# Rearranging the warm-up, the first output tile and the weight loads of a fused attention and feed-forward kernel

## The chip, the cores and the metric

The kernel runs on one core of a Trainium2 chip. The metric is the device time of one execution in microseconds; four runs of the kernel before gave a median of 228.43 us (228.22 to 228.93). The profiled execution is one of these runs.

## The reference

A linear attention with decay (batch 4, 8 heads, 768 positions, head size 64) is followed by a gated feed-forward network (FFN). All inputs and the output are float32.

```python
for b in range(nb):                                  # blocks of 64 positions
    intra = einsum('bhic,bhjc->bhij', qb, kb) * Dmask    # lam ** (i - j), i >= j
    intra = einsum('bhij,bhjd->bhid', intra, vb)
    inter = einsum('bhid,bhde->bhie', qb * lam_pow, kv_state)
    out[:, :, sl] = intra + inter
    kv_state = lam_block * kv_state + einsum('bhsd,bhse->bhde', kb * rev_pow, vb)
x = out.transpose(0, 2, 1, 3).reshape(3072, 512)
g = x @ w_gate                                       # 512 x 1536
return (silu(g) * (x @ w_val)) @ w_out               # 1536 x 512
```

## The kernel before, in words

The 3072 rows of x are worked in six tiles of 512 rows. A tile is two *groups*; a group is 256 positions of one batch element with all heads, so there are twelve groups, 0 to 11. The attention of a group runs ahead of the tile that uses it, in between the FFN's matmuls.

**A group's attention.** `load_group` issues the transfers of k, q and v on SP's queue (`load_fp32`, L93; groups 6 and later in 64-element rows). `cast_scaled` (L255) casts k on ScalarE and scales q on VectorE (in group 3 on GpSimd, called POOL in the profile), and then issues a transposing DMA on SP (`dma_transpose`, L251), which makes the tile qkt. Groups 0 to 2 are transposed on TensorE instead (`pe_transpose`). `v_scale` (L238) makes v_s on GpSimd. On TensorE, `upd_mm` (L382) multiplies k with v_s for the state, `scores` (L326, or L352 from group 6 on) multiplies k with q, `inter` in `core_a` (L461) multiplies q with the state, and `intra` in `core_b` (L474) multiplies the masked scores with v_s. ScalarE copies the update out (`upd_copy`, L404), GpSimd adds it to the state (`state`, L421 to L432), VectorE masks the scores (L333, L357). The masks wait in a list, `later`, and are issued one or two at a time by `run_later` after an FFN step. `guard` (L445) is a tiny ScalarE copy between `inter` and `intra`; `evac` (L486) casts the result into xt, the FFN's input, by default both halves on ScalarE. `ahead(g)` is update and scores of a group; `attend(g)` is `core_a(g)`, then update and scores of the next group, then `core_b(g)`.

**The FFN.** One *step* handles 128 of the 1536 columns: four matmuls for the gate (L514), Silu on ScalarE into a tile sil (L518, three buffers), four matmuls for val (L528) and the product on VectorE into h (L531). Steps of tile 0 and tile 1 are partly halved: 256 rows (`b0` to `b1`) at a time, since the second group comes later. `ffn_out(t, b)` is the last product for 128 rows: twelve matmuls (L547), a copy on ScalarE into osb and a transfer on ScalarE's queue (L549, L550). For the very last one the 512 columns are cut in two: the first half goes over ScalarE, the second over VectorE and SP's queue.

**Weights.** `w_piece` loads pieces of w_gate and w_val, `wo_piece` two row blocks of w_out (512 KB), all on SP's queue and in float32 buffers that they share with k and q (tag raw, ten buffers). `w_cast` and `wo_cast` cast them to bfloat16.

**What sets the order.** Each engine runs its instructions in the order in which they were issued. The order is written out by hand: `step` appends an FFN step to a list, `at(n, fn, ...)` adds a call behind step n, and a loop (L766) issues the steps with their calls. In it, s0 are the steps of tile 0 (from the third on), s1a and s1b those of the two halves of tile 1, sn those of a later tile. PSUM has eight banks that `bank()` hands out in turn, so a bank comes round at every eighth request, and TensorE must wait if the bank's last reader hasn't finished. At the start TensorE is given matmuls on constants (`warm_up`, L130, and `warm_into`, L167), around the product that spreads lam over the partitions (L163), from which ScalarE makes all decay tables by Ln and Exp.

In the kernel before, all of w_out's six pieces are requested behind `s1a[3]`; group 5 is cast behind `s1b[3]`; the outputs of tile 0 stand behind `s1b[11]`, with the attention of group 5 between them, ahead of tile 2:

```python
    at(s1b[11], ffn_out, 0, 0)
    at(s1b[11], ahead, 5)
    at(s1b[11], run_later, 3)
    at(s1b[11], ffn_out, 0, 1)
    at(s1b[11], core_a, 5)
    at(s1b[11], ffn_out, 0, 2)
    at(s1b[11], core_b, 5)
```

Tile 2 then holds the outputs of tile 1, and each later tile those of the one before it.

Of the kernel before, what the change touches and what calls it, by code (L numbers as in the profile page):

```python
# [9 lines left out]
BF16 = mybir.dt.bfloat16  # L10
# [27 lines left out]
def _body(ctx, tc, nc, q, k, v, lam, moe_w_gate, moe_w_val, moe_w_out, out):  # L38
    B, H, S, D = q.shape
    HP = H // 2  # L40
    BLK = 128
    NBLK = S // BLK
    DM = H * D
    DFF = moe_w_gate.shape[1]
    MC = DM // 128
    FC = DFF // 128
    NG = NBLK * B // 2
    M = BLK // 2

# [20 lines left out]
    h_pool = ctx.enter_context(tc.tile_pool(name="h", bufs=2))  # L70
# [8 lines left out]
    def bank():  # L79
        b = banks[ring[0] % 8]  # L80
        ring[0] += 1
        return b
# [8 lines left out]
    st = {}  # L91
# [54 lines left out]
    for b2 in range(2):  # L146
        ps = slice(b2 * M, b2 * M + M)
# [4 lines left out]
    for b2 in range(2):  # L152
        ps = slice(b2 * M, b2 * M + M)
# [5 lines left out]
           for b in range(B)]  # L159

    lam_ps = bank()
    warm_up(4)
    nc.tensor.matmul(lam_ps[:, 0:H], ones[:, 0:128], lam_row, start=True, stop=True)  # L163
    warm_up(3)
    def warm_into(b, n, cols=256):
        for _ in range(n):
            nc.tensor.matmul(b[:, 0:cols], warm[:, 0:128], warm[:, 0:cols], start=True, stop=True)  # L167
# [32 lines left out]
    wv_sb = wpool.tile([128, MC, DFF], BF16, name="wv_sb")  # L200
    wo_sb = wpool.tile([128, FC, DM], BF16, name="wo_sb")
    wg_d = moe_w_gate.rearrange("(c p) f -> p c f", p=128)
# [315 lines left out]
        nc.scalar.activation(sil[:, 0:N], gp[:, 0:N], AF.Silu)  # L518

    def ffn_val(t, fc, b0=0, b1=B):  # L520
        if ("h", t) not in st:
            st[("h", t)] = h_pool.tile([128, FC, B, BLK], BF16, name="h", tag="h")
        h_sb, xt, sil = st[("h", t)], st[("xt", t)], st[("sil", t, fc, b0)]
# [7 lines left out]
        nc.vector.tensor_tensor(out=h_sb[:, fc, b0:b1].rearrange("p b n -> p (b n)"),  # L531
                                in0=sil[:, 0:N], in1=vp[:, 0:N], op=ALU.mult)

    def ffn_fc(t, fc, b0=0, b1=B):
# [1 line left out]
        ffn_val(t, fc, b0, b1)  # L536

    def ffn_out(t, b, last=False):
        h_sb = st[("h", t)]
        osb = osb_pool.tile([128, DM], FP32, name="osb", tag="osb")  # L540
        row = groups[2 * t + b // 2][0] * S + (groups[2 * t + b // 2][1] * 2 + b % 2) * BLK
        halves = ((0, DM // 2, nc.scalar.copy, nc.scalar), (DM // 2, DM, nc.vector.tensor_copy, nc.sync)) \
            if last else ((0, DM, nc.scalar.copy, nc.scalar),)
        for c0, c1, fn, eng in halves:
            ps = bank()[:, 0:c1 - c0]
            for fc in range(FC):
                nc.tensor.matmul(ps, h_sb[:, fc, b], wo_sb[:, fc, c0:c1],  # L547
                                 start=(fc == 0), stop=(fc == FC - 1))
            fn(out=osb[:, c0:c1], in_=ps)  # L549
            eng.dma_start(out=bass.AP(tensor=out.tensor, offset=out.offset + row * DM + c0,  # L550
                                      ap=[[DM, 128], [1, c1 - c0]]),
                          in_=osb[:, c0:c1])
# [3 lines left out]
        upd(g)  # L556
        scores(g)

    def attend(g):
        run_later(len(later))  # L560
        core_a(g)
        if g + 1 < NG:
            upd_mm(g + 1)
            upd_copy(g + 1)
            scores(g + 1)
            late, later[:] = later[:], []
        core_b(g)
# [160 lines left out]
    at(s1b[6], run_later, 2)  # L728
    at(s1b[6], wo_cast)
    at(s1b[6], wo_cast)  # L730
    at(s1b[6], v_scale, 5, nc.gpsimd)
    at(s1b[8], wo_cast)
    at(s1b[9], core_a, 4)
    at(s1b[10], core_b, 4)
    at(s1b[10], wo_cast, ACTC)
    at(s1b[11], ffn_out, 0, 0)
    at(s1b[11], ahead, 5)
    at(s1b[11], run_later, 3)
    at(s1b[11], ffn_out, 0, 1)
    at(s1b[11], core_a, 5)  # L740
    at(s1b[11], ffn_out, 0, 2)
    at(s1b[11], core_b, 5)
    at(s1b[11], cast_scaled, 6)
    at(s1b[11], load_group, 7)
    at(s1b[11], v_scale, 6, nc.gpsimd)
    at(s1b[11], ffn_out, 0, 3)

    outs = [(1, b) for b in range(4)]
    for t in range(2, NG // 2):
        sn = [step(t, fc) for fc in range(FC)]  # L750
        if t == 2:
            at(sn[2], ahead, 6)
        for j, g in ((3 if t == 2 else 0, 2 * t + 3), (7 if t == 2 else 6, 2 * t + 4)):
# [10 lines left out]
        outs = [(t, b) for b in range(4)]  # L764

    for n, (t, fc, b0, b1) in enumerate(steps):  # L766
        if t >= 1 and t + 1 < NG // 2 and ("xt", t + 1) not in st:
# [5 lines left out]
            if fn in (attend, ahead):  # L773
                run_later(1)
    run_later(len(later))
    for t, b in outs:
        ffn_out(t, b, last=(b == 3))
# [1 line left out]
_INS = ['q', 'k', 'v', 'lam', 'moe_w_gate', 'moe_w_val', 'moe_w_out']  # L779
_OUTS = [((3072, 512), 'float32')]  # L780
# [25 lines left out]
```

## Time and profile before

| | |
|---|---|
| median of 4 runs | 228.43 us |
| the profiled execution | 228.93 us |
| its span, first to last instruction | 227.2 us |
| mean granted clock of TensorE | 0.999 |
| TensorE matmuls busy | 218.1 us, 96% of the span |
| ScalarE, GpSimd, VectorE busy | 107.0, 90.0, 89.3 us |
| moved by DMA | 39.70 MB, mean 175 GB/s |

In the profile PE is TensorE, PEld its weight loads, ACT ScalarE, DVE VectorE, POOL GpSimd, SP SyncE, which issues most transfers. L12 is line 12 of the kernel. A busy row gives the busy time of each engine and its instructions; the row of digits cuts the span in 40 slices of 5.68 us, 9 being 90% busy or more. A line of waits gives who waited for whom, and then the total in us, the number of waits and the longest. A line of the chain or of the timeline begins with the start and the duration in us; in the timeline, brackets give the engine's idle time ahead of the instruction and what ended it.

### The profile page before, as it was taken

Reading aid. Unit: us, or ns where it says so; the run is one execution under the profiler, and the core shown is the slowest. Engines: PE = TensorE matmul, PEld = TensorE weight load, DVE = VectorE, ACT = ScalarE, POOL = GpSimd, SP = SyncE. Lnnn points to the kernel's source line nnn. Section 1 sums busy time; section 2 is a strip of 40 time slices with the busy share of each in tenths; the row PEclk is TensorE's granted clock in tenths of the full one; section 3 lists DMA queues with packets and bytes.
Section 4 is the critical chain, followed back from the end, with each engine's and each line's share of the span. In section 5 each row is a group of like instructions: output and inputs, shape, how many; then the busy total and the mean of one; then the engine's idle time right before and its main releaser. Section 6 shows DMA issues by size and latency. Waiting matters only on the chain.

```text
span 227.2 us, 5890 instructions
## 1 busy us (share of the span) xinstructions
PE 218.1 (96%) x2431; PEld 118.2 (52%) x2443; DVE 89.3 (39%) x151; ACT 107.0 (47%) x209; POOL 90.0 (40%) x131
## 2 busy tenths in 40 slices
PE   8789998999998999999999999999999999999994
PEld 3556455878864444454544544544544444444443
DVE  2664357585835214545353362253242123222200
ACT  5878584754662446363354463453433423322221
POOL 6675737732595132978292092092150000000000
PEclk9999999999999999999999999999999999999999
DMA  6999999999997778799977748815101101101122
GB/s 196 345 358 372 367 324 306 229 220 328 349 263 183 203 166 214 185 204 198 225 162 185 189 95 208 218 39 138 49 3 48 46 3 46 46 0 46 49 92 92
DMA packets 88012, 39.70 MB, mean 175 GB/s; under 512 B 57650, under 2 KB 83506, under 8 KB 87986
## 3 DMA queue, kind: packets, MB, share of 16 engines
q1 hardware_dynamic: 83474, 32.64, 54.6%
q10 hardware_dynamic: 4512, 6.69, 8.3%
q8 instruction: 19, 0.31, 0.6%
q14 instruction: 7, 0.06, 0.1%
HBM read 28.31 MB, written 6.29 MB: 152 GB/s over the span
## 4 chain that ended last, share of the span: by engine, by line
PE 73%; DMA 11%; POOL 7%; SPq 5%; issue 1%; ACT 0%; DVE 0%; DVEq 0%; POOLq 0%
PE bank L547 27%; PE bank L514 21%; PE bank L528 20%; DMA v<-in_v_dram 5%; SPq L99 4%; DMA wraw<-in_moe_w_val_dram 4%; DMA woraw<-in_moe_w_out_dram 3%; POOL v_s L238 3%; POOL wo_sb L232 2%; PE bank L474 2%; PE bank L461 2%; PE bank L382 1%; POOL kvf L421 1%; PE bank L352 1%; SPq L227 1%
## 5 line engine op out<-in xcount | busy, mean ns | idle before, releaser
L531 DVE TENSOR_TENSOR h<-sil,bank 128x512 bf16<-128x512 bf16 (+1 forms) x87 | 51.4, 595 | 109.5 <-PE bank L528 93.8
L514 PE MATMUL bank<-xt,wg_sb 128*128 128x512 bf16 (+1 forms) x348 | 76.6, 343 | 0.0
L528 PE MATMUL bank<-xt,wv_sb 128*128 128x512 bf16 (+1 forms) x348 | 76.4, 342 | 0.0
L518 ACT ACTIVATE sil<-bank 128x512 bf16<-128x512 f32 (+1 forms) x87 | 45.9, 527 | 44.2 <-PE bank L514 41.3
L547 PE MATMUL bank<-wo_sb,h 128*128 128x512 bf16 (+1 forms) x288 | 64.3, 370 | 1.5 <-POOL wo_sb L232 0.8
L528 PEld LDWEIGHTS <-wv_sb 128*128 128x128 bf16 x348 | 33.9, 98 | 28.4 <-POOL wv_sb L221 0.3
L514 PEld LDWEIGHTS <-wg_sb 128*128 128x128 bf16 x348 | 32.4, 98 | 27.2 <-DVE xt L486 0.3
L547 PEld LDWEIGHTS <-h 128*128 128x128 bf16 x300 | 29.1, 98 | 33.3 <-issue 1.1
L549 ACT COPY osb<-bank 128x512 f32<-128x512 f32 (+1 forms) x24 | 13.9, 577 | 54.8 <-PE bank L547 52.8
L238 POOL TENSOR_TENSOR v_s<-v,dec 128x1024 bf16<-128x1024 f32 (+1 forms) x14 | 23.3, 1667 | 13.0 <-DMA v<-in_v_dram 9.9
L421 POOL TENSOR_TENSOR kvf<-kvs,ups 128x256 f32<-128x256 f32 x8 | 5.8, 726 | 44.0 <-ACT ups L404 44.0
L333 DVE TENSOR_TENSOR ssb<-bank,causal 128x512 bf16<-128x512 f32 x24 | 15.3, 682 | 3.7 <-PE bank L326 3.6
L486 ACT CAST xt<-bank 128x512 bf16<-128x512 f32 x21 | 12.8, 665 | 2.9 <-PE bank L474 2.4
L430 POOL CAST kvn<-kvf 64x256 bf16<-64x256 f32 x24 | 13.5, 563 | 1.5
L421 POOL TENSOR_TENSOR kvf<-kvf,ups 128x256 f32<-128x256 f32 x16 | 12.6, 787 | 0.6
L404 ACT COPY ups<-bank 128x256 f32<-128x256 f32 (+1 forms) x24 | 9.5, 449 | 2.4 <-PE bank L382 1.5
L258 ACT CAST qk<-kraw 128x1024 bf16<-128x1024 f32 x9 | 9.4, 1043 | 0.0
L260 DVE TENSOR_TENSOR qk<-qraw,qdn 128x1024 bf16<-128x1024 f32 x6 | 7.5, 1255 | 4.1 <-DMA qraw<-in_q_dram 4.1
L357 DVE TENSOR_TENSOR ssb<-bank,causaln 128x512 bf16<-128x512 f32 x12 | 8.2, 687 | 1.2 <-PE bank L352 1.0
L221 POOL CAST wv_sb<-wraw 128x1024 bf16<-128x1024 f32 (+1 forms) x6 | 5.8, 970 | 5.6 <-DMA wraw<-in_moe_w_val_dram 5.4
L232 POOL CAST wo_sb<-woraw 128x1024 bf16<-128x1024 f32 x5 | 5.2, 1043 | 6.3 <-DMA woraw<-in_moe_w_out_dram 6.3
L474 PE MATMUL bank<-ssb,v_s 64*64 64x128 bf16 (+1 forms) x384 | 6.8, 208 | 0.5 <-ACT guard L445 0.5
(63 smaller groups left out, 117.0 us busy)
## 6 DMA issues: line engine op xcount, KB each, us to landing
out_dram<-osb ACTq DMA_DIRECT2D x23, 256.0 KB, 2.1
v<-in_v_dram SPq DMA_DIRECT2D x16, 256.0 KB, 4.5
woraw<-in_moe_w_out_dram SPq DMA_DIRECT2D x6, 512.0 KB, 7.0
kraw<-in_k_dram SPq DMA_DIRECT2D x24, 128.0 KB, 3.3
qraw<-in_q_dram SPq DMA_DIRECT2D x24, 128.0 KB, 3.4
wraw<-in_moe_w_gate_dram SPq DMA_DIRECT2D x5, 512.0 KB, 6.8
wraw<-in_moe_w_val_dram SPq DMA_DIRECT2D x5, 512.0 KB, 7.0
kraw<-in_k_dram SPq DMA_DIRECT2D x4, 512.0 KB, 7.6
```

The costliest lines, as they stand in the source:

```text
L238: eng.tensor_tensor(out=st[("vs", g)][:, h0:h1], in0=st[("v", g)][:, h0:h1].rearrange("p h (s d) -> p h s d", s=2), in1=vfac(g, h0, h1), o ...
L333: nc.vector.tensor_tensor(out=ssb[:, h2, 2 * c:2 * c + 2].rearrange("p a s n -> p a (s n)"), in0=sp[(c, h2)].rearrange("p (a x) -> p a x", ...
L421: nc.gpsimd.tensor_tensor(out=o, in0=f, in1=u, op=ALU.add)
L430: nc.gpsimd.tensor_copy(out=o[64 - h2 * 64:128 - h2 * 64], in_=f[h2 * 64:h2 * 64 + 64])
L474: nc.tensor.matmul(op[r][h2 * 64:h2 * 64 + 64, cols(g, hp, s)], v_s[ps, 2 * hp + h2, s], ssb[ps, h2, hp * 2 + s] if g >= NAT0 else ssb[ps, ...
L486: fns[r](out=xt[:, g % 2, :, r].rearrange("p h (m s) -> p h s m", s=2) if g < NAT0 else xt[:, g % 2, :, :, r * M:r * M + M], in_=op[r].rea ...
L514: nc.tensor.matmul(gp[:, 0:N], wg_sb[:, mc, fs], xt[:, b0 // 2:b1 // 2, mc].rearrange("p g b n -> p g (b n)"), start=(mc == 0), stop=(mc = ...
L518: nc.scalar.activation(sil[:, 0:N], gp[:, 0:N], AF.Silu)
L528: nc.tensor.matmul(vp[:, 0:N], wv_sb[:, mc, fs], xt[:, b0 // 2:b1 // 2, mc].rearrange("p g b n -> p g (b n)"), start=(mc == 0), stop=(mc = ...
L531: nc.vector.tensor_tensor(out=h_sb[:, fc, b0:b1].rearrange("p b n -> p (b n)"), in0=sil[:, 0:N], in1=vp[:, 0:N], op=ALU.mult)
L547: nc.tensor.matmul(ps, h_sb[:, fc, b], wo_sb[:, fc, c0:c1], start=(fc == 0), stop=(fc == FC - 1))
L549: fn(out=osb[:, c0:c1], in_=ps)
```

## The change

Seven edits are made together.

1. The four 512-column matmuls ahead of lam's product become 78 matmuls of 64x64 weights and 8 columns, alternating between the upper and the lower half of the array. Five instead of three wide ones follow.
2. v of group 2 is loaded by two transfers and scaled by two instructions, half of the heads each.
3. Only w_out's first piece is requested behind `s1a[3]`; the other five follow group 5's cast and transpose, which move up from `s1b[3]` to `s1b[0]`. The casts of w_out move later, all to GpSimd.
4. The attention of groups 4 and 5 is regrouped into steps 3 and 8 to 11 of s1b; `attend` can now issue half of the next group's scores.
5. The four outputs of tile 0 move behind step 5 of tile 2. The first step of tile 2 is halved, and the casts, loads, outputs and attention calls of tile 2 get new places. v of group 8 is scaled on VectorE.
6. h is kept in half tiles of six column blocks with five buffers, instead of whole tiles with two.
7. The last output is cut at 384 columns instead of 256.

```diff
     lam_ps = bank()
-    warm_up(4)
+    b = bank()
+    for n in range(78):
+        r = slice(n % 2 * 64, n % 2 * 64 + 64)
+        nc.tensor.matmul(b[r, 0:8], warm[r, 0:64], warm[r, 0:8], start=True, stop=True, skip_group_check=True)
     nc.tensor.matmul(lam_ps[:, 0:H], ones[:, 0:128], lam_row, start=True, stop=True)
-    warm_up(3)
+    warm_up(5)
...
-        halves = ((0, DM // 2, nc.scalar.copy, nc.scalar), (DM // 2, DM, nc.vector.tensor_copy, nc.sync)) \
+        halves = ((0, DM - 128, nc.scalar.copy, nc.scalar), (DM - 128, DM, nc.vector.tensor_copy, nc.sync)) \
...
-    def attend(g):
+    def attend(g, cs=(0, 1)):
...
-            scores(g + 1)
+            scores(g + 1, cs)
...
-    at(s0[4], load_group, 2, "v")
+    at(s0[4], load_fp32, 2, nc.sync, v, "v", 0, H // 2)
+    at(s0[4], load_fp32, 2, nc.sync, v, "v", H // 2, H)
...
-    at(s0[8], v_scale, 2, nc.gpsimd)
+    at(s0[8], v_scale, 2, nc.gpsimd, 0, H // 2)
+    at(s0[8], v_scale, 2, nc.gpsimd, H // 2, H)
...
-    for c in range(0, FC, 2):
-        at(s1a[3], wo_piece, c, c + 2)
+    at(s1a[3], wo_piece, 0, 2)
...
-    at(s1b[3], cast_scaled, 5)
-    at(s1b[3], load_group, 6)
-    at(s1b[4], wo_cast)
-    at(s1b[4], wo_cast)
-    at(s1b[6], ahead, 4)
...
+    at(s1b[0], cast_scaled, 5)
+    for c in range(2, FC, 2):
+        at(s1b[0], wo_piece, c, c + 2)
+    at(s1b[1], v_scale, 5, nc.gpsimd)
+    at(s1b[1], load_group, 6)
+    at(s1b[3], ahead, 4)
+    at(s1b[3], run_later, 2)
+    at(s1b[8], attend, 4, (0,))
+    at(s1b[9], scores, 5, (1,))
+    at(s1b[9], run_later, 2)
+    at(s1b[9], wo_cast)
+    at(s1b[9], wo_cast)
+    at(s1b[10], core_a, 5)
+    at(s1b[11], core_b, 5, SPLIT)
+
     for t in range(2, NG // 2):
         if t == 2:
-            at(sn[2], ahead, 6)
...
+            step(t, 0, 0, 2)
+        sn = [step(t, fc, 2 if fc == 0 and t == 2 else 0) for fc in range(FC)]
+        if t == 2:
+            for n in range(4):
+                at(sn[n], wo_cast)
+            at(sn[4], cast_scaled, 6)
+            at(sn[4], load_group, 7)
+            at(sn[4], v_scale, 6, nc.gpsimd)
+            at(sn[5], ffn_out, 0, 0)
+            at(sn[5], ffn_out, 0, 1)
+            at(sn[5], ahead, 6)
+            at(sn[5], ffn_out, 0, 2)
+            at(sn[5], ffn_out, 0, 3)
+        for j, g in ((6 if t == 2 else 0, 2 * t + 3), (9 if t == 2 else 6, 2 * t + 4)):
             if g < NG:
                 at(sn[j], cast_scaled, g)
                 if g + 1 < NG:
                     at(sn[j], load_group, g + 1)
-                at(sn[1 + j], v_scale, g, nc.gpsimd)
-        if t + 1 < NG // 2:
-            at(sn[6 if t == 2 else 4], attend, 2 * t + 2)
+                if t > 2:
+                    at(sn[1 + j], v_scale, g, nc.gpsimd)
+                else:
+                    at(sn[j], v_scale, g, nc.gpsimd if g == 7 else nc.vector)
+        if t > 2 and t + 1 < NG // 2:
+            at(sn[4], attend, 2 * t + 2)
             at(sn[10], attend, 2 * t + 3)
-        for n, o in zip((0, 3, 7, 9), outs):
-            at(sn[n], ffn_out, *o)
+        for n, b in zip((6, 7, 9, 10) if t == 2 else (0, 3, 7, 9), range(4)):
+            at(sn[n], ffn_out, t - 1, b)
+        if t == 2:
+            at(sn[8], attend, 6)
+            at(sn[10], attend, 7)
```

More of the change, by code (lines that the diff above doesn't have):

```diff
@@ L46, in _body @@
     FC = DFF // 128
+    FH = FC // 2
     NG = NBLK * B // 2
@@ L69, in _body @@
     xt_pool = ctx.enter_context(tc.tile_pool(name="xt", bufs=2))
-    h_pool = ctx.enter_context(tc.tile_pool(name="h", bufs=2))
+    h_pool = ctx.enter_context(tc.tile_pool(name="h", bufs=5))
     sil_pool = ctx.enter_context(tc.tile_pool(name="sil", bufs=3))
@@ L520, in ffn_val @@
     def ffn_val(t, fc, b0=0, b1=B):
-        if ("h", t) not in st:
-            st[("h", t)] = h_pool.tile([128, FC, B, BLK], BF16, name="h", tag="h")
-        h_sb, xt, sil = st[("h", t)], st[("xt", t)], st[("sil", t, fc, b0)]
+        hn = ("h", t, fc // FH)
+        if hn not in st:
+            st[hn] = h_pool.tile([128, FH, B, BLK], BF16, name="h", tag="h")
+        h_sb, xt, sil = st[hn], st[("xt", t)], st[("sil", t, fc, b0)]
         N = (b1 - b0) * BLK
@@ L530, in ffn_val @@
                              start=(mc == 0), stop=(mc == MC - 1))
-        nc.vector.tensor_tensor(out=h_sb[:, fc, b0:b1].rearrange("p b n -> p (b n)"),
+        nc.vector.tensor_tensor(out=h_sb[:, fc % FH, b0:b1].rearrange("p b n -> p (b n)"),
                                 in0=sil[:, 0:N], in1=vp[:, 0:N], op=ALU.mult)
@@ L538, in ffn_out @@
     def ffn_out(t, b, last=False):
-        h_sb = st[("h", t)]
         osb = osb_pool.tile([128, DM], FP32, name="osb", tag="osb")
         row = groups[2 * t + b // 2][0] * S + (groups[2 * t + b // 2][1] * 2 + b % 2) * BLK
-        halves = ((0, DM // 2, nc.scalar.copy, nc.scalar), (DM // 2, DM, nc.vector.tensor_copy, nc.sync)) \
+        halves = ((0, DM - 128, nc.scalar.copy, nc.scalar), (DM - 128, DM, nc.vector.tensor_copy, nc.sync)) \
             if last else ((0, DM, nc.scalar.copy, nc.scalar),)
@@ L546, in ffn_out @@
             for fc in range(FC):
-                nc.tensor.matmul(ps, h_sb[:, fc, b], wo_sb[:, fc, c0:c1],
+                nc.tensor.matmul(ps, st[("h", t, fc // FH)][:, fc % FH, b], wo_sb[:, fc, c0:c1],
                                  start=(fc == 0), stop=(fc == FC - 1))
@@ L722, in _body @@
     at(s1a[10], state, 3)
-    at(s1b[3], cast_scaled, 5)
-    at(s1b[3], load_group, 6)
-    at(s1b[4], wo_cast)
-    at(s1b[4], wo_cast)
-    at(s1b[6], ahead, 4)
[L728 to L748, printed above, removed]
+    at(s1b[0], cast_scaled, 5)
[12 more added lines that the diff above has]
+    at(s1b[11], core_b, 5, SPLIT)
     for t in range(2, NG // 2):
-        sn = [step(t, fc) for fc in range(FC)]
         if t == 2:
-            at(sn[2], ahead, 6)
-        for j, g in ((3 if t == 2 else 0, 2 * t + 3), (7 if t == 2 else 6, 2 * t + 4)):
+            step(t, 0, 0, 2)
[12 more added lines that the diff above has]
+        for j, g in ((6 if t == 2 else 0, 2 * t + 3), (9 if t == 2 else 6, 2 * t + 4)):
             if g < NG:
@@ L757, in _body @@
                     at(sn[j], load_group, g + 1)
-                at(sn[1 + j], v_scale, g, nc.gpsimd)
-        if t + 1 < NG // 2:
-            at(sn[6 if t == 2 else 4], attend, 2 * t + 2)
-            at(sn[10], attend, 2 * t + 3)
-        for n, o in zip((0, 3, 7, 9), outs):
-            at(sn[n], ffn_out, *o)
-        outs = [(t, b) for b in range(4)]
+                if t > 2:
[4 more added lines that the diff above has]
+            at(sn[4], attend, 2 * t + 2)
+            at(sn[10], attend, 2 * t + 3)
+        for n, b in zip((6, 7, 9, 10) if t == 2 else (0, 3, 7, 9), range(4)):
[3 more added lines that the diff above has]
+            at(sn[10], attend, 7)
     for n, (t, fc, b0, b1) in enumerate(steps):
@@ L775, in _body @@
     run_later(len(later))
-    for t, b in outs:
-        ffn_out(t, b, last=(b == 3))
+    for b in range(4):
+        ffn_out(NG // 2 - 1, b, last=(b == 3))
 _INS = ['q', 'k', 'v', 'lam', 'moe_w_gate', 'moe_w_val', 'moe_w_out']
```

## The prediction, made before the result was known

> **What bounds the kernel now.** I read the page's busy rows first, then the list of what TensorE waited for, then the chain of work in order of time, then single stretches. The page:
>
> ```profile
> PE 218.1 (96%) x2431; PEld 118.2 (52%) x2443; DVE 89.3 (39%) x151; ACT 107.0 (47%) x209; POOL 90.0 (40%) x131
> ...
> DMA  6999999999997778799977748815101101101122
> ```
>
> TensorE sets the time from about 37 us on; the DMA engines are full (nines) from 6 to 68 us. What TensorE waited for (us in total, times, longest):
>
> ```profile
> PE bank L547 <- POOL wo_sb L232: 0.8, 1, 0.8
> PE bank L167 <- issue: 0.6, 1, 0.6
> ...
> PE bank L382 <- POOL v_s L238: 0.5, 1, 0.5
> ```
>
> Three idle spots, all before 70 us. The chain up to 38 us (start, us, what) shows what the early ones are worth:
>
> ```profile
> 16.95 8.02 DMA wraw<-in_moe_w_val_dram
> ...
> 28.65 6.63 DMA v<-in_v_dram
> 35.27 0.07 issue
> 35.34 1.93 POOL v_s L238
> 37.27 0.04 issue
> 37.31 0.45 PE bank L382 x32
> ```
>
> Until 37.31 the chain is transfers and the casts behind them: the update of group 2 starts when POOL has scaled v of group 2, which landed at 35.27. TensorE itself was ready at about 36.7. The other stretches (start, us, instruction):
>
> ```profile
> 59.15 6.27 SPq L251 DMA_TRANSPOSE qkt<-qk  x1
> ...
> 65.71 1.33 ACT L486 CAST xt<-bank 128x512 bf16<-128x512 f32 x2 [0.58 <-PE bank L474]
> ...
> 69.14 1.02 PE L547 MATMUL bank<-wo_sb,h 128*128 128x512 bf16 x4 [0.78 <-POOL wo_sb L232]
> ```
>
> ```profile
> DMA to landing us min/median/max: 3.7/4.8/9.9
> ```
>
> The first output tile stops at 67.99 for the last piece of w_out; with the matmul's own length the loss is 0.93 us (the 12 matmuls and the switch to attention take 3.61 us from 66.48 to 70.09, against 2.59 + 0.09). The transposing DMA of group 5 holds SP's queue for 6.27 us behind six weight pieces, landing 9.9 us after its issue, the maximum of the last line (tile qkt); the median is 4.8 us.
>
> **What the Trainium skill says.** "TensorE: Matmul & The Clock Gate", Back-to-back issue gap: N/2.4 + 2.5 ns per matmul; the trace agrees (four of 512 columns in 0.863 us, 215.8 ns each; 16 transposes of 128 columns in 0.89 us, 56 ns). Same page, Part 1: the clock is halved until about 3.4 us of activity; here 512-column matmuls stand 427 ns apart up to about 4.8 us. "Runtime: NRT & Kernel Launch", Instruction fetch mechanics: instructions come in blocks of 256, 16 KiB, fetched by DMA, mostly hidden; the page's queue list has 19 instruction packets with 0.31 MB, 16.3 KB each, and the 0.6 us of "issue" at 14.1 us ends 1.2 us after the first of them (12.57 to 13.53). "DMA: Bandwidth & Descriptors", Queues, rings and completion order: a ring's descriptors are taken in order; the 9.9 us of group 5's transpose fit.
>
> **The change part by part.** The sum is against the profiled execution, 228.93 us (span 227.2 and 1.7 around it); its median of runs is 228.43, so I apply the difference to that.
>
> *Start.* Four 427 ns matmuls become 78 tiny ones. The trace has no such matmul at half clock. Low end: 8 ns apiece, like the 64x64 groups of L382 at full clock (32 in 0.27 us), 0.6 us, and the product then waits for lam, landed at 1.98. High end: one weight load of 64 columns at 1.2 GHz each, in series, 53 ns, 4.1 us. I take about 20 ns (two row groups alternate), so the product starts near 2.4 instead of 2.64. ScalarE's Ln started at 3.27, after a table load that ends at 3.11: at most 0.16 us earlier. Then k of group 0 lands at 4.60, and later steps wait for v of group 1 (landed 12.14, scaled until 13.46). The five warm-ups after it end near 4.7 as now. 152 more instructions move the fetch boundary (now at TensorE's 449th instruction) to work of about 11 us, with the fetch asked for long before: the 0.64 us at 14.1 go. That buys nothing: val of fc 2 starts at 20.35 because POOL's cast of its weights ends at 20.29, which waited for its transfer. Value 0; at the high end the product is 2.4 us later, of which the waits above cover most, cost up to 1 us.
>
> *Group 2's v in two halves.* POOL is free at 34.84. Half casts take 1.05 us (four in the trace): 34.84 + 2 x 1.05 = 36.94 instead of 37.25. **-0.31** (0 if the first half lands later than 35.2, -0.6 if the wait went altogether). The second DMA instruction on SP (about 0.7 us of issue) sits ahead of k and q of group 3, whose transpose has 1.7 us of margin.
>
> *Outputs of tile 0 inside tile 2.* w_out's casts now stand ten microseconds ahead of their use: **-0.93**. SP's five pieces, now behind group 5's transpose and not before it, land near 68; first use is near 80. 9 stays of attention between FFN steps become 8, each switch costing 0.09 in and 0.13 out: **-0.22**. The halved first step of tile 2 costs 0.02; five half-size h buffers instead of two whole ones cost nothing, as h of tile 0's halves must live until sn[5].
>
> *Group 5's transpose.* q lands at 55.23, DVE's cast takes 1.22, the transpose is issued near 56.5 and lands after 4.2 to 6.1 us, at 60.7 to 62.6; its scores come near 63.4. Hidden. DVE's wait for q holds h of three half steps for about 1 us, which eight banks and three sil buffers cover.
>
> *A new wait for banks in s1b[8] to s1b[10].* Let P be the end of step s1b[8]. attend(4,(0,)) takes two banks for op, two for up, two for scores; step s1b[9] the next two; scores(5,(1,)) again op's two. These are free when ScalarE has copied them: intra starts at P+1.25, the copies 0.69 later (as 65.02 to 65.71), 1.33 long: P+3.27. TensorE is there at P+1.25+0.57+0.45+0.53 = P+2.80. **+0.48**. sil of s1b[9] stands behind these copies (3.65), h behind it (4.11), a mask of scores behind h (4.8), and core_a(5), ready at 4.6, wants that mask's bank: **+0.20**. Bounds 0.3 and 1.0 together.
>
> *Two tight transposes in tile 2.* T is the end of sn[4]. h ends at T+0.97, q's cast at T+2.22, the transpose of group 6 is issued at T+2.36; with 3.7 to 5.5 us it lands at T+6.1 to 7.9. Its scores are due after sn[5] (1.73), two outputs (5.18), 0.36: T+7.28. **+0.1** (0 to 0.6). Group 7's is issued at T+17.75 (a mask, 0.68, is ahead of the cast). k, q of group 8 follow in SP's queue; in the trace q's last packet came 10.2 to 12.0 us after such an issue, so q lands at T+28.3 to 29.7. DVE's cast is in turn at T+28.2, ends near 29.6, the transpose issued at 29.75 lands at 34.55 by the median. scores(8) is due in attend(7) at T+34.1. **+0.5** (0 to 2.6). Behind DVE's waiting cast stand v_scale of group 8 (1.25, v near T+31) and h of sn[10]; both are done before T+33. Group 9's loads come 2 to 3 us later than now, its scores have over 3 us of margin.
>
> *End.* The last tile's second part is 128 columns instead of 256: TensorE's sum is equal (12 x 162.5 + 12 x 55.8 ns against 24 x 109.2, both 2.62 us). Now:
>
> ```profile
> 223.93 0.42 DVE L549 COPY osb<-bank 128x256 f32<-128x256 f32 x1 [9.69 <-DMA out_dram<-osb]
> 224.38 0.38 SPq L550 DMA_DIRECT2D out_dram<-osb  x1
> ```
>
> The copy falls from 0.42 to about 0.27 (128x512 costs 0.73, so 0.31 per 256 columns), the transfer from 1.76 to about 1.6 us (256 KB takes 1.97): **-0.27** (-0.1 to -0.35). ScalarE's larger part (0.48 copy) is issued 0.5 us sooner and lands before it.
>
> Sum: -0.31 - 0.93 - 0.22 - 0.27 + 0.02 + 0.48 + 0.20 + 0.1 + 0.5 = **-0.43**; 228.43 - 0.43 = 228.0 us.
>
> **The rivals.** *The waits for transposes don't come* (chance 0.25): with 3.7 us, as in the trace at 135.71 with idle DMA engines, both land in time, and half of the bank wait goes: -1.73 + 0.02 + 0.4 = -1.3, 227.1 us. For it: output transfers are the only other traffic then. Against: q of group 8 itself.
>
> *The transpose of group 8 becomes the bound and makes it slower* (0.22). Place: scores(8) in attend(7). q 12.0 us after the issue and a transpose of 5.5 us (both in the trace) make the wait 2.6 us instead of 0.5; half of that excess gives +0.6, 229.0, all of it +1.7, 230.1. From a wait of 0.93 us on, the kernel is slower than before. Against: three of five such transposes took 4.7 to 4.9 us.
>
> *The start slips* (0.08). If tiny matmuls don't hold the clock up, full speed comes one or two 3.4 us windows later. One window is covered by waits of 1.8 us between 5.7 and 9; two would double about 3 us of dense work, less the 0.64 of fetch wait: near +1 after the other gains, 229.4. In this case the change doesn't do what it says. *A fetch lands late* (0.03) in the dense stretch near 64 us: +0.5, 228.9. The forecast has 0.42, its own range 227.6 to 228.5.
>
> **How the numbers follow.** A measurement can tell about 0.2%, 0.46 us. Faster: the first rival, and almost half of the forecast's share, 0.44. Within: the other half and some of the later cases, 0.28. Slower: 0.28. The range 226.9 to 229.4 leaves out the deepest gain and the longer waits for group 8.
>
> **What would show it.** In the profile after: no wait of L547 for wo_sb; the wait for v_s near 0.3; a wait of L326 for ScalarE's xt of about 0.5 near 65 us; L352 waiting after the upd of group 8 near 112 us, its size deciding the sign; the last copy at 0.27. Wrong would be a later end of half-speed matmuls, idle "issue" time over 0.3 us, or a first full step of tile 0 that starts later than now.

## The result and the profile after

The changed kernel is slower. Its median is 230.62 us (228.65 to 235.01, 40 runs) against 228.49 us for the kernel before (227.81 to 231.48, 61 runs). The ratio is 1.0069, 95% interval 1.0053 to 1.0085; runs more than 1.5% above the fastest of their kernel are left out of it, so it is smaller than the ratio of the medians. The forecast was 228.0, 0.43 us less than before; the ratio stands for 1.6 us more. Four more profiles of the changed kernel come further down; the first, of 229.8 us (span 228.1), answers to the lines shown of before. Its line numbers are some four higher. The page:

```profile
PE 220.2 (97%) x2515; PEld 121.2 (53%) x2527; DVE 91.1 (40%) x154; ACT 105.5 (46%) x208; POOL 88.6 (39%) x132
...
DMA  6999999999899259699779857835101101101122
```

TensorE is busy 2.1 us longer, 1.15 us of it in the first 16 us (13.99 against 12.84). The waits of TensorE (total, times, longest, us):

```profile
PE bank L533 <- POOL wv_sb L645: 0.6, 1, 0.6
...
PE bank L356 <- DMA qkt<-qk: 0.4, 1, 0.4
...
PE bank L330 <- ACT xt L490: 0.3, 1, 0.3
...
PE bank L533 <- POOL wv_sb L225: 0.2, 1, 0.2
```

The waits for w_out, for v_s and for instructions at 14 us are gone, as the change meant. New are waits for weights of val in the first tile (wv_sb), for group 8's transpose and for the bank. The chain of work, in order of time:

```profile
7.46 2.20 SPq L100
9.70 0.65 SPq L217
...
13.30 7.57 DMA wraw<-in_moe_w_val_dram
20.92 1.05 POOL wv_sb L225
22.02 1.04 PE bank L533 x4
```

Up to 22 us it consists of SP's requests, one weight transfer and its cast; behind that it is TensorE almost throughout. So the loss lies in the start: the update of group 2 begins at 38.37 instead of 37.31 (+1.06), and TensorE ends at 224.81 instead of 223.84 (+0.97). The timeline at the places shown of before (start, length, idle time ahead of it in brackets):

```profile
57.59 1.64 SPq L255 DMA_TRANSPOSE qkt<-qk  x1
...
65.27 1.33 ACT L490 CAST xt<-bank 128x512 bf16<-128x512 f32 x2
...
66.65 0.41 PE L330 MATMUL bank<-qkt 64*64 64x128 bf16 x15 [0.27 <-ACT xt L490]
...
80.55 1.67 PE L551 MATMUL bank<-wo_sb,h 128*128 128x512 bf16 x6
...
224.90 0.29 DVE L553 COPY osb<-bank 128x128 f32<-128x128 f32 x1 [9.69 <-DMA out_dram<-osb]
225.22 0.38 SPq L554 DMA_DIRECT2D out_dram<-osb  x1
```

Group 5's transpose holds SP for 1.64 us instead of 6.27; the first output starts without a wait (80.55); the bank wait at 66.65 is there; the last copy took 0.29 us. The transposing DMAs (tile qkt) no longer have one of 9.9 us:

```profile
DMA to landing us min/median/max: 3.7/3.8/5.8
```

**What happens in the start.** TensorE's own instructions arrive by DMA. In the kernel before the first packet in the profile comes at 12.57 us, the next at 18.42 and 28.64; in the changed kernel they come at 7.78, 13.43 and 19.84, since 152 instructions more stand ahead. Every data transfer of the start is cut in 16 parts. In the kernel before, the 16 parts of the second half of k of group 1 complete between 9.43 and 9.85 us. After, 15 complete between 9.41 and 9.78 and the last at 11.00. The next transfers are alike: 15 parts of q by 10.52, the last at 11.75; of v by 11.30 and 12.52. So one sixteenth of every transfer runs some 1.2 us late behind the fetch. The kernel before shows the same from 12.57 us (15 parts of a weight piece by 13.60, the last at 15.06), when the data of groups 0 and 1 have landed. All other profiles but one show it too: in the transfers that end within one to four microseconds of the first fetch, the last part comes 1.0 to 2.0 us behind the other 15 (in `b_tiny2` 0.6 to 0.8). A request of SP, which takes about 0.7 us otherwise, is then held up; before, and after:

```profile
8.50 0.69 SPq L213 DMA_DIRECT2D wraw<-in_moe_w_gate_dram  x1
...
12.18 2.10 SPq L213 DMA_DIRECT2D wraw<-in_moe_w_val_dram  x1
```

```profile
6.77 2.89 SPq L100 DMA_DIRECT2D v<-in_v_dram  x2
...
14.04 2.57 SPq L217 DMA_DIRECT2D wraw<-in_moe_w_gate_dram  x1
```

The first weight request leaves at 9.70 instead of 8.50. The val weights of the first full step of tile 0 are complete at 20.87 instead of 19.20, and their cast and the matmuls follow at once. Before (after stands in the chain above, at 20.92 and 22.02):

```profile
19.25 1.04 POOL L221 CAST wv_sb<-wraw 128x1024 bf16<-128x1024 f32 x1 [2.05 <-DMA wraw<-in_moe_w_val_dram]
...
20.35 1.04 PE L528 MATMUL bank<-xt,wv_sb 128*128 128x512 bf16 x4
```

That is 1.67 us. What was moved in the first 20 us, before and after:

```profile
DMA packets 10396, 6.17 MB, mean 309 GB/s; under 512 B 305, under 2 KB 10394, under 8 KB 10394
```

```profile
DMA packets 9926, 5.72 MB, mean 286 GB/s; under 512 B 295, under 2 KB 9923, under 8 KB 9923
```

The granted clock is late too: full from 8.51 us, not from 4.93. Three candidates for the start's loss had to be separated: the fetches, the clock, and TensorE being 1.2 us later at its first transposes (5.64 instead of 4.42).

### The profile page after: what moved, and what is told of

The parts are those of the page before. It is cut to its first block, busy times and chain, and to the rows that moved or that the text cites. A ratio compares the mean times of both kernels' runs of the same rounds, so it can differ in the third digit from the quotient of the medians.

```text
span 228.1 us, 6067 instructions
## 1 busy us (share of the span) xinstructions
PE 220.2 (97%) x2515; PEld 121.2 (53%) x2527; DVE 91.1 (40%) x154; ACT 105.5 (46%) x208; POOL 88.6 (39%) x132
## 4 chain that ended last, share of the span: by engine, by line
PE 85%; SPq 5%; DMA 5%; ACT 1%; issue 1%; POOL 0%; ACTq 0%; DVE 0%; DVEq 0%
PE bank L518 26%; PE bank L533 26%; PE bank L551 26%; SPq L100 4%; DMA wraw<-in_moe_w_val_dram 3%; DMA qkt<-qk 2%; PE bank L478 2%; PE bank L465 2%; SPq L217 1%; PE bank L386 1%; PE bank L330 1%; PE bank L356 1%; ACT xt L490 1%; POOL wv_sb L225 0%; PE bank L293 0%
## 5 line engine op out<-in xcount | busy, mean ns | idle before, releaser
L551 PE MATMUL bank<-wo_sb,h 128*128 128x512 bf16 (+2 forms) x289 | 64.2, 370 | 0.6
L242 POOL TENSOR_TENSOR v_s<-v,dec 128x1024 bf16<-128x1024 f32 (+1 forms) x14 | 22.2, 1598 | 18.5 <-DMA v<-in_v_dram 8.7
L337 DVE TENSOR_TENSOR ssb<-bank,causal 128x512 bf16<-128x512 f32 x24 | 15.5, 683 | 2.9 <-PE bank L330 2.7
L490 ACT CAST xt<-bank 128x512 bf16<-128x512 f32 x20 | 12.2, 661 | 2.4 <-PE bank L478 2.4
L434 POOL CAST kvn<-kvf 64x256 bf16<-64x256 f32 x24 | 11.6, 483 | 1.5
L478 PEld LDWEIGHTS <-v_s 64*64 64x64 bf16 x384 | 5.5, 105 | 1.6 <-issue 1.4
```

The costliest lines, as they stand in the source:

```text
L242: eng.tensor_tensor(out=st[("vs", g)][:, h0:h1], in0=st[("v", g)][:, h0:h1].rearrange("p h (s d) -> p h s d", s=2), in1=vfac(g, h0, h1), o ...
L337: nc.vector.tensor_tensor(out=ssb[:, h2, 2 * c:2 * c + 2].rearrange("p a s n -> p a (s n)"), in0=sp[(c, h2)].rearrange("p (a x) -> p a x", ...
L434: nc.gpsimd.tensor_copy(out=o[64 - h2 * 64:128 - h2 * 64], in_=f[h2 * 64:h2 * 64 + 64])
L478: nc.tensor.matmul(op[r][h2 * 64:h2 * 64 + 64, cols(g, hp, s)], v_s[ps, 2 * hp + h2, s], ssb[ps, h2, hp * 2 + s] if g >= NAT0 else ssb[ps, ...
L490: fns[r](out=xt[:, g % 2, :, r].rearrange("p h (m s) -> p h s m", s=2) if g < NAT0 else xt[:, g % 2, :, :, r * M:r * M + M], in_=op[r].rea ...
L551: nc.tensor.matmul(ps, st[("h", t, fc // FH)][:, fc % FH, b], wo_sb[:, fc, c0:c1], start=(fc == 0), stop=(fc == FC - 1))
```

## Experiments

Ratios are to the kernel before on the same chip, with 95% intervals. The *lead* of a kernel is its matmuls on constants ahead of and right behind lam's product; the old lead is that of the kernel before.

### Edit 1 alone, and everything but edit 1

`b_tiny` is the kernel before with edit 1. `a_oldlead` is the changed kernel with edit 1 undone:

```diff
-    b = bank()
-    for n in range(78):
-        ...
+    warm_up(4)
     nc.tensor.matmul(lam_ps[:, 0:H], ones[:, 0:128], lam_row, start=True, stop=True)
-    warm_up(5)
+    warm_up(3)
```

> The kernel before with edit 1 alone (78 tiny matmuls, lam's product, five wide ones). Start theory (the loss comes from edit 1): full clock near 8.5 us instead of 4.9, first transposes 1.2 us later, and a time 1.2 to 1.9 us above the kernel before, as much as all edits together lose. Rival (the loss comes from the new waits in tiles 1 and 2): within 0.3 us of the kernel before.

> The changed kernel with the four wide matmuls, lam's product and the three wide ones of the kernel before in place of edit 1. Start theory: full clock near 4.9 us and a time 0.2 to 0.6 us below the kernel before, since the other edits are then worth the sum of the prediction. Rival (waits in tiles 1 and 2): still 1 us or more above the kernel before.

`b_tiny`: 229.59 against 228.12 us, ratio 1.0065 (1.0040 to 1.0091). `a_oldlead`: 228.87 against 228.12, ratio 1.0026 (1.0007 to 1.0044). Edit 1 alone loses about what all seven edits lose. But the other six aren't a gain either, 0.75 us between the medians: neither theory had that number.

### Clock, fetches or a late TensorE

`b_lam5` drops the matmuls ahead of lam's product, `b_fetch` adds instructions at no TensorE time, `b_late` makes TensorE late, `b_tiny2` is edit 1 without the lateness:

```diff
 b_lam5, a_lam5 (on the kernel before, on the changed one): nothing ahead of lam's product, then
+    warm_up(5)
 b_late, on the kernel before:
-    warm_up(3)
+    warm_up(7)
 b_tiny2: edit 1, but
-    warm_up(5)
+    warm_up(2)
 b_fetch, on the kernel before:
-    warm_up(4)
+    warm_up(32, 64)
...
-    warm_up(3)
+    warm_up(24, 64)
+    (28 tiny matmuls between 5.9 and 9 us)
```

> The kernel before without any matmul ahead of lam's product, and five wide ones behind it: four instructions fewer than before, so TensorE's instruction fetches stay where they are, and only the clock can come later. Clock theory: full speed near 8.5 us and 0.9 to 1.5 us above the kernel before. Fetch theory (the loss comes from instruction fetches that move into the crowded start): within 0.4 us of the kernel before.

> The kernel before with its seven wide matmuls cut into 56 of 64 columns and 28 tiny matmuls put into waits between 6 and 9 us: 154 instructions more, about as many as edit 1 adds, at no more TensorE time. Clock theory: full speed near 4.9 us and within 0.3 us of the kernel before. Fetch theory: TensorE's first instruction fetch moves from 12.6 us to about 6.6 us, SP's issues and the landings from 9 us on are 1 us or more late, and the time is 0.5 to 1.5 us above the kernel before.

> The kernel before with seven wide matmuls behind lam's product, not three: TensorE's first transposes come about 1.2 us later, as with edit 1, but the clock comes early and only 8 instructions are added. Theory of the late TensorE (edit 1 costs what TensorE is late): 1.0 to 1.4 us above the kernel before. Fetch theory: within 0.4 us of it, since waits for data behind it cover the delay.

> The kernel before with edit 1, but with two wide matmuls behind lam's product, not five: the first transposes come within 0.4 us of the kernel before, while 146 instructions are added ahead of them. Theory of the late TensorE: within 0.5 us of the kernel before. Fetch theory: first fetch of instructions near 8 us, landings from 9 us on 1 us late, and 1.0 us or more above the kernel before.

> The changed kernel without the 78 tiny matmuls: lam's product first, then five wide ones, so TensorE's fetches of instructions stay where the kernel before has them, while full clock still comes late, as in b_lam5. Fetch theory: it wins back most of what edit 1 costs, a median within 0.4 us of a_oldlead (0.4 to 0.9 us above the kernel before). Clock theory: it stays 1.4 us or more above the kernel before, as the changed kernel.

| kernel | first transposes | full clock | first fetch | moved in 20 us | ratio |
|---|---|---|---|---|---|
| before | 4.42 us | 4.93 us | 12.57 us | 6.17 MB | 1 |
| b_lam5 | 4.74 | 8.43 | 13.12 | 6.26 | 1.0010 (0.9993 to 1.0027) |
| b_late | 5.96 | 5.77 | 13.24 | 6.22 | 1.0012 (0.9997 to 1.0027) |
| b_tiny2 | 4.59 | 8.52 | 7.91 | 5.62 | 1.0043 (1.0026 to 1.0061) |
| b_fetch | 4.33 | 4.19 | 9.32 | 5.74 | 1.0079 (1.0044 to 1.0115) |
| b_tiny | 5.64 | 6.90 | 7.94 | 5.64 | 1.0065 (1.0040 to 1.0091) |
| a_lam5 | 4.75 | 6.07 | 12.27 | 6.25 | 1.0024 (1.0007 to 1.0040) |
| changed | 5.64 | 8.51 | 7.78 | 5.72 | 1.0069 (1.0053 to 1.0085) |

The second to fifth columns are readings of one profile each. The loss goes with the fourth and fifth. A late clock alone and a late TensorE alone have ratios that can't be told from 1, though a cost of up to 0.27% is within their intervals and their medians are higher (228.95 against 228.12 us, between what the two theories said, and 228.90 against 228.48). The single runs are plainer: 36 of 55 runs of the kernel before are below 228.6 us, 6 of 22 of `b_lam5`, and none of the 14 of `b_tiny` or the 10 of `b_fetch`; on the other chip 36 of 67, 10 of 22 of `b_late`, none of the 22 of `b_tiny2`. So the clock and the lateness may cost some tenths of a microsecond, and the added instructions cost more, in `b_fetch` without either of the two. Edit 1 with TensorE on time (`b_tiny2`, 229.75 us) still loses 0.43%. With the clock early as well, instructions alone (`b_fetch`, 230.35 us) cost 0.79%; TensorE is on time there too, its first update beginning at 9.40 us (9.43 before). Its first fetch came at 9.32 us, later than I had expected, and cost no less than in `b_tiny`. Its waits, in a profile that is the longest of its ten runs (232.08 us), name the weights:

```profile
PE bank L535 <- POOL wv_sb L224: 2.3, 2, 1.8
```

`a_lam5` takes only the 78 tiny matmuls out of the changed kernel's lead and lands where `a_oldlead` does (229.27 us, 1.0024 and 1.0026). From 1.0069 this is 0.45%, 1.0 us: the price of the tiny matmuls in the changed kernel. The clock of `a_lam5` came early in its profile (6.07 us), so it doesn't by itself exclude the clock as the main cause; `b_lam5` and `b_fetch` do that.

The update of group 2 shows that the loss arises in the start. In the changed order it begins at 36.42 to 36.67 us in five profiles without the tiny matmuls (a sixth, `a_ahead2`, has 38.18, with the clock halved again from 15.10 to 18.52 us), and at 37.15 to 38.67 in the seven with them. So the +1.06 us above is what is left of some 1.7 us (38.37 against 36.66 in `a_oldlead`) after the gain of edit 2.

### The transposing DMAs of groups 6 to 8

The profile of `a_oldlead` was a long one, 235.19 us, and showed where these edits are fragile. Its largest wait of TensorE:

```profile
PE bank L353 <- DMA qkt<-qk: 4.1, 2, 3.8
```

Group 6's transpose was issued at 81.97, a fetch of instructions came at 84.11, nearly nothing was moved from 84.4 to 86.0, and it landed at 88.84, after 6.9 us. The clock was then halved from 87.93 to 94.75 us. Four variants start these transfers earlier:

```diff
 a_oldlead_t6 (old lead) and a_t6 (changed lead):
-            at(sn[4], cast_scaled, 6)
+            at(sn[3], cast_scaled, 6)
 a_t6_t8, on a_oldlead_t6 (v of group 8 stays behind sn[6]):
+            at(sn[4], load_group, 8, "kq")
 a_ahead, on a_t6_t8 (v of group 7 stays behind sn[4]):
+            at(sn[2], load_group, 7, "kq")
```

> The changed kernel with the lead of the kernel before (as in a_oldlead) and group 6 cast behind step 3 of tile 2, not step 4, so that its transposing DMA starts some 3 us earlier. Theory of group 6 (in a_oldlead this DMA landed 3.8 us after TensorE wanted it, which also took the clock down for 6.8 us; so it is what costs the 0.7 us): no wait of the scores for it, 0.2 to 0.7 us below the kernel before, and times close together. Rival (edits 2 to 7 lose elsewhere): still 0.4 us or more above the kernel before.

> The changed kernel with group 6 cast behind step 3 of tile 2, not step 4, and nothing else. Theory of group 6: it loses about 1 us less than the changed kernel, 0.6 to 1.3 us above the kernel before, which is what edit 1 costs, and without times above 232 us. Rival (edit 1 is the whole loss): as the changed kernel, 1.4 us or more above the kernel before.

> a_oldlead_t6 with k and q of group 8 requested behind step 4 of tile 2, ahead of group 7's transposing DMA on SP, not behind step 6. Theory of group 8 (in a_oldlead_t6 TensorE waits 1.1 us for group 8's transposing DMA, whose q landed only at 107.4 us, because its transfer was requested behind group 7's transposing DMA): that wait goes, and the time is 0.2 to 0.8 us below the kernel before. Rivals: the wait moves to group 7's transposing DMA, which now stands behind eight transfers (no gain on a_oldlead_t6), or the loss lies elsewhere (0.4 us above the kernel before or more).

> a_t6_t8 with k and q of group 7 requested earlier as well, behind step 2 of tile 2, so that every load stands one transposing DMA further ahead. Theory of group 8: no wait for a transposing DMA of groups 6 to 8, 0.4 to 1.0 us below the kernel before, the fastest so far. Rival: the transfers in front of group 6's transposing DMA make that one late, 0.3 us or more above the kernel before.

| kernel | median, before | ratio | in the profile |
|---|---|---|---|
| a_oldlead_t6 | 229.03, 228.48 us | 1.0015 (0.9994 to 1.0036) | none for group 6, 1.07 us for group 8 |
| a_t6 | 230.43, 228.48 | 1.0065 (1.0042 to 1.0087) | 0.32 us for group 8 |
| a_t6_t8 | 232.11, 228.41 | 1.0158 (1.0129 to 1.0186) | 2.36 us for group 7, 0.71 for group 8, clock halved 103.56 to 106.97 |
| a_ahead | 228.52, 228.41 | 1.0009 (0.9993 to 1.0024) | 0.18 us for group 8 |

The waits in this table and the next are counted from the start of the last matmul ahead; the idle time in brackets, which begins at its end, is 0.19 us shorter.

`a_t6` refutes that group 6 carries the changed kernel's loss. It was also to be without times above 232 us, and 4 of its 22 runs are above (6 of 40 of the changed kernel, none of the 27 of `a_oldlead_t6` and `a_ahead`), so group 6 alone doesn't make the long runs either. `a_oldlead_t6` is no faster than the kernel before: the time went on to group 8,

```profile
112.82 0.45 PE L353 MATMUL bank<-qkt 64*64 64x64 bf16 x32 [0.89 <-DMA qkt<-qk]
```

which doesn't come earlier with TensorE, since its q is requested behind group 7's transpose. `a_t6_t8` moves the wait to group 7, as its rival said. Only with all loads one transpose ahead is TensorE's idle time ahead of these scores gone: in `a_ahead`'s profile TensorE ends at 223.42, 0.41 us before the kernel before. Its median is nevertheless no lower than that kernel's.

### The two kernels once more, and the bank wait alone

`a_ahead2` divides the evacuation of group 4 over two engines; `before_2` and `after_2` are the two kernels unchanged.

```diff
-        core_b(g)
+        core_b(g, SPLIT if g == 4 else (ACTC, ACTC))
```

> The kernel before, profiled once more. Theory of the reference run (the sum of the prediction was made against a profile whose waits were longer than in most runs of the kernel before, so edits 2 to 7 removed less than it says): span 226.2 to 226.7 us, not 227.2, and the waits of TensorE for wo_sb, v_s and its own instructions together at least 0.5 us shorter than the 2.2 us of the first profile. Rival: the same waits again, within 0.2 us.

> The changed kernel, profiled once more. Theory (what varies in it are the start, with its weights that land late, and the transposing DMAs of groups 6 to 8, each of which can land after TensorE wants it): where the span differs from the 228.1 us of the first profile by 0.5 us or more, the difference stands in waits for weights before 35 us or in waits for qkt between 80 and 115 us. Rival: it stands elsewhere, in waits for w_out or for PSUM banks.

> a_ahead with the evacuation of group 4 divided between VectorE and ScalarE, in place of both halves on ScalarE. The wait of the second half of group 5's scores for ScalarE's xt, 0.5 us of TensorE idle near 64.5 us in every profile of the changed order, should go: 0.3 to 0.5 us below a_ahead, 0.1 to 0.5 us below the kernel before. Rival: the idle time moves to the next wait behind it (the fetch of instructions near 67.5 us), no gain on a_ahead.

`before_2` took 230.38 us (span 228.7): longer, against my theory. Its wait for w_out is 1.8 us, where the first profile had 0.8. The other profiles of the old order have 0.4 (`b_lam5`), 1.8 (`b_late`), 0.4 (`b_tiny2`), 0.2 (`b_tiny`) and 0.2 (`b_fetch`). So this wait isn't a fixed 0.93 us, and mostly the later TensorE starts group 2, the shorter it is: 36.75 us in `before_2`, 37.31, 37.82, 38.31, 38.70 and 40.69 in `b_fetch`; `b_late` is the exception, with 39.21: its profile is that of a 232.35 us run, the longest of its 22, in which the clock was halved again from 16.01 to 19.43 us. `a_ahead2`: 228.87 against 228.74 us, ratio 1.0013 (0.9986 to 1.0040). Its bank wait is gone, but its profile, one of its longer runs (230.75 us), waits for instructions instead,

```profile
PE bank L530 <- issue: 1.6, 1, 1.6
```

up to 70.53 us; `a_ahead` has 0.3 of this at 68.08. No gain is shown.

`after_2` took 231.19 us. TensorE ends as in the first profile (224.85, against 224.81), but the end of the span comes 4.6 us later instead of 3.3. A twentieth fetch at 226.36 us falls into the last transfer: 15 of its parts complete by 226.89, the last at 228.38. The kernel before has 19 fetches, the last at 212 us; in the changed kernel's first profile the twentieth came at 228.47, after the end. One run tested whether this explains the high median (68 tiny matmuls need no twentieth fetch), and three more profiles of the changed kernel followed:

```diff
-    for n in range(78):
+    for n in range(68):
```

> The changed kernel with 68 tiny matmuls, not 78: its TensorE program is 20 instructions shorter, about as long as that of b_tiny, and should end with the nineteenth fetch of instructions. Theory of the last fetch (the changed kernel alone needs a twentieth, and where it falls into the last output transfer, as in its second profile at 226.4 us, one of the 16 parts of that transfer ends 1.5 us late): no fetch after 200 us, 3.1 to 3.4 us from TensorE's end to the end of the span, and 0.5 to 0.9 us less than the changed kernel loses, so 0.7 to 1.1 us above the kernel before. Rival (the early fetches alone): as the changed kernel, 1.4 to 1.8 us above the kernel before.

> The changed kernel, third profile. Start theory: where its time is above 230.3 us, TensorE waits longer for weights before 35 us (over 1.5 us, against 0.8 us in the first profile). Theory of group 6: there it waits for group 6's transposing DMA near 85 us, or a clock reduced after such a wait. Rival: neither, but the output's end or w_out.

> The changed kernel, fourth profile, with the same question: a time above 230.3 us stands in waits for weights before 35 us (start), in group 6's transposing DMA near 85 us with the clock behind it, or elsewhere.

> The changed kernel, fifth profile, with the same question: a time above 230.3 us stands in waits for weights before 35 us (start), in group 6's transposing DMA near 85 us with the clock behind it, or elsewhere.

`a_tiny68` has 19 fetches and 3.15 us from TensorE's end to the end of the span, but its median is 231.27 against 228.76 us, ratio 1.0099 (1.0065 to 1.0132). The last fetch is a real cost in the runs it hits and not the cause of the median. The five profiles of the changed kernel:

| profile | time | full clock | update of group 2 | waits for groups 6 and 8 | TensorE ends | to the end of the span |
|---|---|---|---|---|---|---|
| first | 229.80 us | 8.51 us | 38.37 us | 0, 0.62 us | 224.81 us | 3.29 us |
| after_2 | 231.19 | 6.45 | 38.43 | 0, 0.27 | 224.85 | 4.63 |
| after_3 | 235.42 | 8.21 | 38.67 | 2.06, 2.59 | 230.56 | 3.16 |
| after_4 | 229.68 | 7.19 | 38.28 | 0, 0.24 | 224.68 | 3.16 |
| after_5 | 228.57 | 8.43 | 37.15 | 0, 0.55 | 223.59 | 3.16 |

`after_3` is one of the long runs. Its waits for transposes:

```profile
88.51 0.45 PE L356 MATMUL bank<-qkt 64*64 64x64 bf16 x32 [1.87 <-DMA qkt<-qk]
...
117.90 0.65 PE L356 MATMUL bank<-qkt 64*64 64x64 bf16 x32 [2.41 <-DMA qkt<-qk]
```

The clock was halved from 117.44 to 120.85 us, and TensorE worked from 117.90 on: half of 2.95 us is 1.5, an estimate. With 2.06, with 2.59 - 0.62 and with 0.30 for the later group 2 that is 5.8 us, the whole distance of TensorE's end from the first profile (5.75). `after_5` is the opposite: full clock late at 8.43, fetches early, but the second fetch took 0.89 us, not 1.90 as in the first profile. SP's request took 1.3 us there, not 2.6, TensorE waited for no weights, and group 2 came at 37.15, ahead of the kernel before, though still behind the 36.66 of the old lead. It moved

```profile
DMA packets 10082, 5.85 MB, mean 293 GB/s; under 512 B 300, under 2 KB 10080, under 8 KB 10080
```

in 20 us, between the two kernels. So a late clock doesn't prevent a good start. That the weights decide is what the waits in the other profiles say.

## Why the prediction was wrong, step by step

**Start: the step that failed.** It was valued at 0, at most 1 us for slow tiny matmuls. It costs about 1.0 us in the changed kernel (1.0069 against 1.0024, with an uncertainty of about half of that) and 0.65% alone. This is half of the 2.0 us between the forecast of -0.43 and the 1.6 measured; the other half is in the sum, below. The prediction saw the fetch move "to work of about 11 us, with the fetch asked for long before: the 0.64 us at 14.1 go", and that was right; the changed kernel's TensorE doesn't wait for the fetch. It left out that the fetch is itself a DMA in a full queue. The Trainium skill's "Runtime: NRT & Kernel Launch", Instruction fetch mechanics, calls the crossing "mostly hidden", and I carried this over from TensorE to the DMA engines, where it doesn't hold: 1.2 us on one of 16 parts of each transfer. The weights' transfer, on which the prediction rested the value of 0, came later itself: val of the first full step began at 22.02, not 20.35. Of the prediction's signs of being wrong, the later first full step and the later end of half speed came true clearly, and idle "issue" time over 0.3 us by a hair (0.33 us at 3.9). The price of a tiny matmul was near the assumed 20 ns: 78 in 2.1 us, 27 ns apiece, and lam's product at 3.02 instead of 2.64.

**The rival of the slipping start** named the right place and nearly the size (+1), by the wrong mechanism; that the size fits is luck. The clock did come later, as it said. The Trainium skill's "TensorE: Matmul & The Clock Gate", Part 1, says that the window runs freely, so that the ramp varies between runs; the profiles agree, 6.45 to 8.51 us in five of one kernel. But it costs little beside the fetches: the start's waits for data cover most of it (`b_lam5`, `after_5`). "Covered by waits of 1.8 us" was right to some tenths of a microsecond.

**Group 2's v, w_out.** Both waits went, as said. Taking -0.31 and -0.93 as fixed sizes was the second mistake: w_out's wait is a buffer, 0.2 to 1.8 us long, that takes up what happens ahead of it. The wait for v_s comes and goes as well: `before_2` has none and starts group 2 at 36.75, as early as the profiles with edit 2 and the old lead (36.66). In the changed kernel both waits are gone, and what the other waits and switches gain and lose behind group 2 about cancels (+1.06 at group 2, +0.97 at TensorE's end).

**Group 5's transpose, the bank wait.** It landed at 62.98, a little after the 62.6 of the range, and hidden. The bank wait was 0.50 us (0.48 said). The second part of 0.20, for a mask's bank, didn't come.

**Groups 6 and 8.** Group 8 waited 0.24 to 0.62 us in four of five profiles (0.5 said). Group 6's +0.1, with 0.6 as upper end, holds for these four; 2.06 us in `after_3` and 3.97 in `a_oldlead` lie outside. With a fetch in their midst, a transpose took 6.9 us in `a_oldlead` and one 6.5 in `a_oldlead_t6`; without one, those of groups 6 to 8 took 3.7 to 6.1. No run shows by itself that the fetch makes the difference. The clock was halved around the longest of these waits. These rare long waits belong in a price.

**End.** -0.27 was said; from TensorE's end to the end of the span it is 3.38 before and 3.16 to 3.29 after, -0.09 to -0.22, except where the twentieth fetch adds 1.3.

**The sum.** Without edit 1, the six edits came to +0.26% (0.07 to 0.44) and, with the transposes in time, +0.09% (-0.07 to 0.24), not to -0.43 us. For `a_ahead`, which has no idle time for groups 6 and 8, the prediction's terms without their 0.6 us make -1.03. Between the two profiles it is -0.63 (spans 227.2 and 226.6; a wait of 0.3 for instructions at 68.08, which the prediction held to be rare, is part of the gap), and between the medians +0.11. The profile of before (228.93) was 0.5 us slower than the median from which I subtracted, and its waits are what the terms remove. Whether the kernel before has shorter waits in its median run, I can't show: its second profile was a still longer run. So why these six edits gain nothing stays open in part. Open, too, is what share of the changed kernel's distance between median and first profile (0.8 us) each of the three variable places has. No version tried beats the kernel before.

## What to carry to other kernels

Where the DMA engines are full, as they were here in the start, count instructions as traffic: look up in the trace when an engine's instruction packets are fetched, and which transfers are in flight then. Filler matmuls should be few and wide. A wait for data that stands behind an improvement or a loss is a buffer and not a constant: take its length from several profiles, and ask what reaches the end once it is gone.

## What the runs showed of the hardware

- An instruction fetch of 16 KB takes 0.88 to 2.1 us in the crowded start, and the last of 16 parts of the next transfers then comes 1.0 to 2.0 us after the other 15 (19 of 20 profiles). The request that SP has in issue at the first fetch takes 1.7 to 2.4 us in all 20, against about 0.7 for those around it. The Trainium skill's "DMA: Bandwidth & Descriptors", Queues, rings and completion order, has a copy split over up to 16 rings, which fits the one late part.
- 64x64 matmuls of 8 columns didn't raise the clock in these runs: full speed came at 6.45 to 9.04 us in the nine profiles that begin with them, at 6.07 and 8.43 in the two with nothing in their place, and at 4.57 to 6.01 in the eight that begin with 512-column ones. With 128x128 matmuls of 64 columns it came at 4.19 in the one profile that has them.
- Stops of TensorE of 2.41 and 2.18 us went with a halved clock over 3.41 us (`after_3`, `a_t6_t8`), one of 3.79 us with 6.83 us (`a_oldlead`). The length alone doesn't decide: behind 1.19 us in `b_late`, at 15.5, the clock was halved as well, behind 1.76 to 1.87 us in `before_2`, `b_fetch` and `after_3` it wasn't.
